# Experts taken in the order of their token counts, with a room of their own rank each (gate loop attention, then top-1 routed experts)

## The chip, the cores and the metric

The kernel runs on one core of one Trainium2 chip. The metric is the device time of one execution in microseconds (us), the median of several executions. The profile is of one execution; its span runs from the first to the last instruction, and its own time is a little longer than the span.

## What is computed

The first half is a gated linear recurrence, 4 batches of 8 heads, 768 tokens, head size 48. The second half sends each of the 3072 tokens (384 values) to one of 8 experts.

```python
for t in range(S):                       # attention
    new_re = ar * S_re - ai * S_im;  new_im = ar * S_im + ai * S_re
    S_re, S_im = (new_re + kv, new_im)
    y[:, :, t] = einsum('bhd,bhde->bhe', q[:, :, t], S_re)
logits = x @ w_gate                      # x: (3072, 384), 8 experts
expert_idx = argmax(logits, axis=1);  gate_w = probs[arange(N), expert_idx]
for e in range(E):                       # w1[e]: (384, 1024), w2[e]: (1024, 384)
    out[mask] = gate_w[mask, None] * (maximum(x[mask] @ w1[e], 0) @ w2[e])
```

## The kernel before

**Two stages.** In the attention stage (`front`, `chunk`, `route`) the work is cut into units of 128 to 384 tokens. ScalarE (ACT) and VectorE (DVE) turn gates, queries and keys of a unit into the operand `zp`; SyncE (SP) moves it by DMA into `hz`; then TensorE (PE) works through chunks of 128 tokens. When enough chunks are done, `route` finds each token's expert and its place in that expert's room, and GpSimd (POOL) scatters the rows to the DRAM buffer `xs_hbm` (L495). Every expert has a room of `CAP` = 448 rows there; rows from `MINC` = 256 on are filled beforehand with empty rows by three DMAs (L528).

**The expert stage.** For expert e, `weights` loads the two weight matrices (`w1b`, `w2b`, 1536 KB each, three buffers of each), `tokens` loads the expert's room in four DMAs (`xb`, L617), and DVE transposes it into `xrt` (L629). Then come 8 groups of 3 matmuls, each 448 columns wide (L644), into one of five PSUM banks; ACT and DVE in turn apply the relu and write `ht`. The second matmul (L658) works in three tiles of 128 tokens, 8 matmuls of 384 columns each. The last 64 rows of two neighbouring experts share one tile (L670): the two experts' matmuls write the two halves of the output's 128 partitions. Each output tile is scaled by its gate on DVE (L602) and scattered to the output by POOL (L591).

**What sets the order.** Both stages are lists of operations with guessed durations in a `Plan`; `Plan.order` tries list schedules with random priorities, keeps the one with the shortest guessed span, and the instructions are issued in that order, engine by engine. ACT holds one table at a time; the attention plan has two kinds of ACT operation, and at each change of kind a table is loaded (L540). The plan of the expert stage starts where the attention plan ends; on SP the first weight loads stand after the last `hz` DMA.

**The guard.** From the final counts and some bounds the kernel computes a flag (`again`, L544 to L568). If an expert has more rows than its room or fewer than `MINC`, a slow path (from L691) computes everything again. It isn't run with these inputs: the final counts of the eight experts, worked out from the reference, are 354, 406, 392, 388, 370, 421, 338 and 403.

Of the kernel before, what the change touches and what calls it, by code (L numbers as in the profile page):

```python
# [30 lines left out]
CAP = 448  # L31
# [3 lines left out]
NB = CAP // 32  # L35
# [12 lines left out]
class Plan:  # L48
# [48 lines left out]
    def run(self, prio, edges, ins, back, stick):  # L97


        ops, n = self.ops, [len(x) for x in ins]  # L100
        ready, start = [0.0] * len(ops), [0.0] * len(ops)
        cur, dma = None, 0.0
        port, other = {"DVE": 0.0, "POOL": 0.0}, {"DVE": "POOL", "POOL": "DVE"}
        free, cand = {o["eng"]: 0.0 for o in ops}, {o["eng"]: [] for o in ops}
        for o in ops:
            if n[o["i"]] == 0:
                cand[o["eng"]].append(o["i"])
        for _ in ops:
            pick = None
            for eng, cs in cand.items():  # L110
                if not cs:
                    continue
                f = free[eng]
                fp = max(f, port[other[eng]]) if eng in port else f
                at = [max(fp if ops[i]["port"] else f, ready[i]) for i in cs]
                low = min(at)
                if pick is not None and low >= pick[2]:
                    continue
                best = None
                for i, t in zip(cs, at):  # L120
                    if t <= low + self.SLACK:
                        sw = ops[i]["tag"] and cur and ops[i]["tag"] != cur
                        key = prio[i] - (stick if sw else 0.0)
                        if best is None or key > best[0]:
                            best = (key, i, t + (self.TBL if sw else 0.0))
                if pick is None or best[2] < pick[2]:
                    pick = (eng, best[1], best[2])
            eng, i, t = pick
            o = ops[i]
            cand[eng].remove(i)  # L130
            start[i] = t
            free[eng] = issued = end = t + o["dur"] * (self.PE[t > self.PE[2] or back] if eng == "PE" else 1.0)
            if o["port"]:
                port[eng] = end
            cur = o["tag"] or cur
            if o["wire"] and not back:
                dma = end = max(dma, end) + o["wire"]
            for s, us, data in edges[i]:
                ready[s] = max(ready[s], end + us + (ops[s]["wire"] if back else 0.0) if data else issued)
                n[s] -= 1  # L140
                if n[s] == 0:
                    cand[ops[s]["eng"]].append(s)
        return start, max(free.values())
# [19 lines left out]
def gateloop_then_moe(ctx, tc, gates, qk, v, wg, w1, w2, out):  # L163
# [50 lines left out]
    ones_b = const([128, 128], "ones_b", 1.0, BF16)  # L214
    cum = const([128, E], "cum")
# [7 lines left out]
    with ExitStack() as att:  # L223
# [277 lines left out]

        def setup():
# [14 lines left out]
        with tc.manual_schedule():  # L517
            for u in range(NU):
# [7 lines left out]
                if u == 3:  # L526
                    for h in range(3):
                        P.add("SP", 0.65, lambda h=h: nc.sync.dma_start(  # L528
                            xs_hbm.rearrange("(e s) w -> s e w", e=E)[MINC + 64 * h:MINC + 64 * h + 64],
                            bc(empty[0:64, None, :], [64, E, W])), (), (("empty", h),), lat=2, wire=3.2, after=moved[1])  # L530
                for c in range(t0 // 128, t1 // 128):
                    chunk(b, c, t1 - t0 == TU)
                    for r0, r1 in ROUTES[b]:
                        if r1 == c + 1:
                            route(b, r0, r1)
            for i in P.order():
                o = P.ops[i]
                if o["tag"] and o["tag"] != getattr(P, "cur", None):
                    P.cur = o["tag"]
                    nc.scalar.preload_act_table_set("natural_log_exp_and_others" if P.cur == "LE" else "trig_and_small")  # L540
                o["fn"]()
# [20 lines left out]
    nc.vector.tensor_scalar(out=f4, in0=f4, scalar1=float(CAP), scalar2=None, op0=ALU.is_le)  # L562
# [8 lines left out]
    with ExitStack() as ms:  # L571
# [4 lines left out]
        NW = 3  # L576
        w1b = buf("w1b", NW, [128, DT * F])
        w2b = buf("w2b", NW, [128, FT * DM])
        xrt = buf("xrt", 2, [128, DT, CAP])
        ht = buf("ht", 2, [128, FT, CAP])  # L580
        yo = buf("yo", 4, [128, DM])
        hg = buf("hg", 2, [128, 2])
        xb = buf("xb", 2, [128, NB, 96])
        gi = buf("gi", 2, [128, 3, 2])
        HB, OB = bank[0:5], bank[5:8]
        M = Plan()
# [19 lines left out]
        def weights(e):  # L606
            ws = e % NW
            M.add("SP", 0.65, lambda: nc.sync.dma_start(w1b[ws], w1[e * 128:e * 128 + 128, :]), (), (("w1", ws),), lat=1.9, wire=5.2,
                  after=rows[-1:])
            M.add("SP", 0.65, lambda: nc.sync.dma_start(w2b[ws], w2[e * 128:e * 128 + 128, :]), (), (("w2", ws),), lat=1.9, wire=5.2,  # L610
                  after=rows[-1:])

        def tokens(e, s):

            for i in range(4):
                eng, dma = ("ACT", nc.scalar) if e == 0 and i % 2 else ("SP", nc.sync)
                j = M.add(eng, 0.65, lambda i=i, dma=dma: dma.dma_start(  # L617
                    xb[s][32 * i:32 * i + 32], xs_hbm[e * CAP:(e + 1) * CAP, 104 * i:104 * i + 96].rearrange("(j p) w -> p j w", p=32)),
                    ("routed",), (("xb", s, i),), lat=2.5 if e == 0 else 6.0, wire=0.9)
            if e:  # L620
                rows.append(j)
            z, hgi = e % 2, e // 2 % 2
            M.add("SP", 0.65, lambda: nc.sync.dma_start(
                gi[s], xs_hbm[e * CAP:e * CAP + 384, XW:W].rearrange("(j p) w -> p j w", p=128)), ("routed",), (("gi", s),), lat=3.0, wire=0.5)
            M.add("SP", 0.65, lambda: nc.sync.dma_start(
                hg[hgi][64 * z:64 * z + 64], xs_hbm[e * CAP + 384:(e + 1) * CAP, XW:W]), ("routed",), (("hg", hgi, z),), lat=3.0, wire=0.1)
            for j in range(4):
                b0, b1 = 4 * j, min(4 * j + 4, NB)
                M.add("DVE", (b1 - b0) * 96 * 0.00105 + 0.1, lambda b0=b0, b1=b1: nc.vector.transpose(  # L629
                    xrt[s][:, :, 32 * b0:32 * b1].rearrange("p d (b t) -> p b d t", t=32),  # L630
                    xb[s][:, b0:b1].rearrange("p b (d c) -> p b d c", d=DT)), tuple(("xb", s, i) for i in range(4)), (("xrt", s, j),))

        def expert(e):
            s, ws = e % 2, e % NW
            if e > 1:
                weights(e)
            tokens(e, s)
            for f_ in range(FT):
                hb = (e * FT + f_) % 5

                def f(f_=f_, hb=hb):
                    for d in range(DT):
                        c = d * F + f_ * 128
                        nc.tensor.matmul(HB[hb][:, 0:CAP], lhsT=w1b[ws][:, c:c + 128], rhs=xrt[s][:, d, :], start=(d == 0), stop=(d == DT - 1))  # L644
                M.add("PE", 2.28, f, (("w1", ws),) + tuple(("xrt", s, j) for j in range(4)), (("H", hb),))
                if f_ % 2:
                    M.add("DVE", 0.6, lambda f_=f_, hb=hb: nc.vector.tensor_scalar_max(ht[s][:, f_, :], HB[hb][:, 0:CAP], 0.0),  # L647
                          (("H", hb),), (("ht", s, f_),))
                else:
                    M.add("ACT", 0.6, lambda f_=f_, hb=hb: nc.scalar.activation(ht[s][:, f_, :], HB[hb][:, 0:CAP], func=ACT.Relu),  # L650
                          (("H", hb),), (("ht", s, f_),))
            for j in range(3):
                ob = cnt["o"] % 3
                cnt["o"] += 1
                for a in range(2):
                    def f(j=j, ob=ob, a=a):
                        for f_ in range(4 * a, 4 * a + 4):
                            nc.tensor.matmul(OB[ob][:, 0:DM], lhsT=ht[s][:, f_, j * 128:j * 128 + 128], rhs=w2b[ws][:, f_ * DM:f_ * DM + DM],  # L658
                                             start=(f_ == 0), stop=(f_ == FT - 1))
                    M.add("PE", 2.6, f, (("w2", ws),) + tuple(("ht", s, f_) for f_ in range(4 * a, 4 * a + 4)), (("O", ob),))  # L660
                finish(ob, gi[s][:, j, 0:1], gi[s].bitcast(I32)[:, j, 1:2], (("gi", s),))
            hgi = (e // 2) % 2
            if e % 2:
                ob = cnt["o"] % 3
                cnt["o"] += 1

                def f(ob=ob):
                    for f_ in range(FT):
                        for z in range(2):
                            nc.tensor.matmul(OB[ob][64 * z:64 * z + 64, 0:DM], lhsT=ht[z][:, f_, 384:CAP],  # L670
                                             rhs=w2b[(e - 1 + z) % NW][:, f_ * DM:f_ * DM + DM], start=(f_ == 0), stop=(f_ == FT - 1),
                                             skip_group_check=True)
                rd = tuple(("ht", z, f_) for z in range(2) for f_ in range(FT)) + (("w2", (e - 1) % NW), ("w2", e % NW))
                M.add("PE", 5.3, f, rd, (("O", ob),))
                finish(ob, hg[hgi][:, 0:1], hg[hgi].bitcast(I32)[:, 1:2], (("hg", hgi, 0), ("hg", hgi, 1)))

        with tc.manual_schedule():
            weights(0)
            weights(1)
# [162 lines left out]
```

## Time and profile before

| what | value |
|---|---|
| three runs, median (lowest to highest) | 575.65 us (570.49 to 575.82) |
| profiled execution, its own time | 571.32 us |
| its span | 569.6 us, mean granted TensorE clock 0.927 |
| busy: PE, DVE, ACT, POOL | 477.8, 280.2, 184.1, 113.2 us |
| first L644 matmul starts | 271.62 us |
| last scatter (L591) starts | 564.38 us |

Busy time is a mean over two stages with different limits, so the stages are read apart below: which engine is full in each, and what the others wait for.

### The profile page before, as it was taken

What the parts mean: (1) busy time and instruction counts of PE and PEld (TensorE: products, weight loads), DVE (VectorE), ACT (ScalarE), POOL (GpSimd) and SP (SyncE); (2) the same over time, 40 slices, a digit from 0 to 9 for tenths busy, and PEclk for the clock granted to TensorE, in tenths of its full rate; (3) what the DMA queues carried; (4) which work ended last, traced back from release to release, by engine and by line L of the source; (5) the groups of instructions that cost most, each with busy time, mean ns of one, the idle gap of its engine ahead of it and who ended that gap; (6) DMA issues with size and microseconds to landing.
All of it is one profiled execution on the core that took longest, in us unless ns stands there. A gap on an engine that the chain in (4) does not pass through costs nothing. (4 is left out here: it accounts for less than half of the span.)

```text
span 569.6 us, 6957 instructions
## 1 busy us (share of the span) xinstructions
PE 477.8 (84%) x2689; PEld 324.0 (57%) x2689; DVE 280.2 (49%) x449; ACT 184.1 (32%) x259; POOL 113.2 (20%) x116
## 2 busy tenths in 40 slices
PE   0254766988697989881999999999999999999995
PEld 0244666877696878780455545555455554555552
DVE  7999999999899999342212021022011120200201
ACT  6784776767586756240100000100000000000100
POOL 6342214026303521421000001010021010100202
PEclk9966868898799889896899999999999999999999
DMA  8755675759999664695936063067343300400101
GB/s 275 222 187 149 194 221 154 226 148 312 266 260 223 182 175 112 235 397 120 274 71 159 28 171 138 3 239 181 52 152 126 111 29 1 138 14 0 47 10 48
DMA packets 48424, 86.15 MB, mean 151 GB/s; under 512 B 22512, under 2 KB 37904, under 8 KB 46336
## 3 DMA queue, kind: packets, MB, share of 16 engines
q1 hardware_dynamic: 43840, 75.19, 45.7%
q0 software_dynamic: 3328, 9.86, 4.7%
q10 hardware_dynamic: 1216, 0.59, 0.5%
q8 instruction: 23, 0.38, 0.3%
q14 instruction: 17, 0.14, 0.1%
HBM read 54.32 MB, written 13.21 MB: 119 GB/s over the span
## 5 line engine op out<-in xcount | busy, mean ns | idle before, releaser
L644 PE MATMUL bank<-xrt,w1b 128*128 128x448 f32 x384 | 150.1, 544 | 9.5 <-DVE xrt L629 9.5
L658 PE MATMUL bank<-w2b,ht 128*128 128x384 f32 x384 | 128.4, 487 | 0.0
L644 PEld LDWEIGHTS bank<-xrt,w1b 128*128 128x128 f32 x384 | 73.5, 192 | 78.9 <-issue 63.0
L658 PEld LDWEIGHTS bank<-w2b,ht 128*128 128x128 f32 x384 | 72.7, 190 | 54.3 <-issue 10.3
L400 PE MATMUL bank<-hz 128*128 128x128 f32 x384 | 65.1, 325 | 45.3 <-DMA hz<-zp 33.0
L650 ACT ACTIVATE ht<-bank 128x448 f32<-128x448 f32 x32 | 17.4, 545 | 253.9 <-PE bank L644 227.2
L400 PEld LDWEIGHTS bank<-hz 128*128 128x128 f32 x384 | 57.7, 231 | 50.1 <-DVE cs L330 25.3
L591 POOL DMA_INDIRECT out_dram<-yo,gi x24 | 23.5, 980 | 270.5 <-DVE yo L602 245.5
L647 DVE TENSOR_SCALAR ht<-bank 128x448 f32<-128x448 f32 x32 | 20.0, 624 | 93.9 <-PE bank L644 89.5
L602 DVE TENSOR_SCALAR yo<-bank,gi 128x384 f32<-128x384 f32 x24 | 14.8, 617 | 96.6 <-PE bank L658 91.8
L176 DVE TENSOR_TENSOR zp<-Z,cs 128x1152 f32<-128x1152 f32 (+2 forms) x40 | 45.2, 1169 | 0.1
L176 POOL TENSOR_TENSOR AB<-AB,C 128x1152 f32<-128x1152 f32 (+2 forms) x9 | 21.2, 2352 | 96.9 <-ACT C L264 89.7
L176 DVE TENSOR_TENSOR am<-bank,causal 128x512 f32<-128x512 f32 x48 | 32.0, 681 | 16.8 <-PE bank L400 10.8
L419 PE MATMUL bank<-am,v 128*48 128x128 f32 x384 | 30.4, 297 | 9.4 <-DVE am L176 9.2
L435 PE MATMUL bank<-turn,yt 128*128 128x104 f32 x192 | 29.2, 300 | 10.7 <-ACT yt L423 7.8
L495 POOL DMA_INDIRECT xs_hbm<-xg,slot x24 | 27.7, 1154 | 36.4 <-issue 14.9
L629 DVE STREAM_TRANSPOSE xrt<-xb 128x384 f32<-128x384 f32 (+1 forms) x32 | 14.0, 497 | 40.2 <-PE bank L644 32.7
L435 PEld LDWEIGHTS bank<-turn,yt 128*128 128x128 f32 x192 | 25.8, 209 | 13.1 <-ACT yt L423 8.5
L427 PE MATMUL bank<-v,kt 128*96 128x48 f32 x320 | 32.3, 257 | 0.0
L427 PEld LDWEIGHTS bank<-v,kt 128*96 128x96 f32 x320 | 30.7, 174 | 1.8 <-issue 1.5
L176 POOL TENSOR_TENSOR Z<-Z,AB 128x1152 f32<-128x1152 f32 (+2 forms) x9 | 21.7, 2407 | 41.8 <-ACT AB L264 41.7
L540 ACT ACT_TABLE_LOAD x23 | 29.5, 1283 | 1.2 <-PEq L830 0.8
(111 smaller groups left out, 479.1 us busy)
## 6 DMA issues: line engine op xcount, KB each, us to landing
w1b<-in_w_dram SPq DMA_DIRECT2D x8, 1536.0 KB
w2b<-in_w_dram SPq DMA_DIRECT2D x8, 1536.0 KB
hz<-zp SPq DMA_DIRECT2D x24, 432.0 KB
AB<-in_gates_dram SPq DMA_DIRECT2D x12, 576.0 KB
Z<-in_qk_dram SPq DMA_DIRECT2D x12, 576.0 KB
xb<-xs_hbm SPq DMA_DIRECT2D x30, 168.0 KB
v<-in_v_dram SPq DMA_DIRECT2D x8, 576.0 KB
xs_hbm<-empty SPq DMA_DIRECT2D x3, 836.0 KB
```

What stands on the lines that cost most here:

```text
L176: (eng or nc.vector).tensor_tensor(out=o, in0=a, in1=b, op=op)
L400: nc.tensor.matmul(SC[hf][:, (h % 4) * 128:(h % 4) * 128 + 128], lhsT=hk[:, h], rhs=hq[:, h], start=True, stop=True)
L419: nc.tensor.matmul(YT[ps, (h // 2) * 128:(h // 2) * 128 + 128], lhsT=V[:, cl, h * D:h * D + D], rhs=am[2 * par + hf][:, h % 4, :], start=( ...
L427: nc.tensor.matmul(ST[0:96, h * D:h * D + D], lhsT=kt[par][:, h * 96:h * 96 + 96], rhs=V[:, cl, h * D:h * D + D], start=(c == 0 and h == 0 ...
L435: nc.tensor.matmul(XT[:, p * 104:p * 104 + 104], lhsT=yt[par][:, p * 128:p * 128 + 128], rhs=turn[:, p, :], start=True, stop=True)
L495: i = nc.gpsimd.indirect_dma_start(out=xs_hbm[:, :], out_offset=bass.IndirectOffsetOnAxis(ap=R[slot][:, c:c + 1], axis=0), in_=xg[:, (g0 + ...
L540: nc.scalar.preload_act_table_set("natural_log_exp_and_others" if P.cur == "LE" else "trig_and_small")
L591: i = nc.gpsimd.indirect_dma_start(out=out[:, :], out_offset=bass.IndirectOffsetOnAxis(ap=index, axis=0), in_=y, in_offset=None, bounds_ch ...
L644: nc.tensor.matmul(HB[hb][:, 0:CAP], lhsT=w1b[ws][:, c:c + 128], rhs=xrt[s][:, d, :], start=(d == 0), stop=(d == DT - 1))
L647: M.add("DVE", 0.6, lambda f_=f_, hb=hb: nc.vector.tensor_scalar_max(ht[s][:, f_, :], HB[hb][:, 0:CAP], 0.0), (("H", hb),), (("ht", s, f_),))
L650: M.add("ACT", 0.6, lambda f_=f_, hb=hb: nc.scalar.activation(ht[s][:, f_, :], HB[hb][:, 0:CAP], func=ACT.Relu), (("H", hb),), (("ht", s, ...
L658: nc.tensor.matmul(OB[ob][:, 0:DM], lhsT=ht[s][:, f_, j * 128:j * 128 + 128], rhs=w2b[ws][:, f_ * DM:f_ * DM + DM], start=(f_ == 0), stop= ...
```

## The change

Experts are taken in the order of their counts. A new function `ranks`, run when all but the last 384 tokens are routed, sorts the counts on DVE; the result `order` holds the expert of each rank. SP (and ACT for the first expert) loads the expert's number into a register, and the DMAs of weights, tokens and gates take their address from it. Each rank has its own room (`CAPS`): 480, 448, 416, 416, 416, 384, 384, 384; they are worked through in the turns 0, 2, 1, 3 to 7. The room in `xs_hbm` is 480 rows for every expert. Rows past 384 are collected 32 at a time from several experts in two shared tiles of four parts each (`SHARED`), one finished with the second turn and one with the fifth. There are four buffers of `w2b` and three of `ht`; `weights` is called for one expert ahead of the loop, not for two. The three DMAs of empty rows cover 224 rows in place of 192. The planner gets one more rule (`landed`): a transfer that SP or ACT issues starts when the eighth last one has landed. The guard compares the counts by rank with `CAPS`.

```diff
-CAP = 448
+CAP = 480
+CAPS = (480, 448, 416, 416, 416, 384, 384, 384)
+TURNS = (0, 2, 1, 3, 4, 5, 6, 7)
+SHARED = ((1, ((0, 384, 0), (0, 416, 32), (0, 448, 64), (1, 384, 96))), (4, ((2, 384, 0), (2, 416, 32), (3, 384, 64), (4, 384, 96))))
...
-                at = [max(fp if ops[i]["port"] else f, ready[i]) for i in cs]
+                at = [max(fp if ops[i]["port"] else f, ready[i], landed[-8] if ops[i]["wire"] and eng != "POOL" else 0.0) for i in cs]
...
+        def ranks():
+            cnt = bank[2][:, 440:440 + E]
+            P.add("PE", 0.3, lambda: nc.tensor.matmul(cnt, lhsT=ones_b, rhs=cumb, start=True, stop=True), ("cumb",), ("RT",))
...
+            dv(lambda: tt(key, cnt, keyb, ALU.subtract), ("RT",), ("key",))
+            dv(lambda: tt(tmp, bc(key[:, None, :], full), bc(key[:, :, None], full), ALU.is_le), ("key",), ("tmp",))
+            dv(lambda: nc.vector.tensor_reduce(above, tmp, axis=AX, op=ALU.add), ("tmp",), ("above",))
+            dv(lambda: tt(pick, bc(above[:, None, :], full), bc(rev[:, :, None], full), ALU.is_equal), ("above",), ("pick",))
+            dv(lambda: tt(tmp, pick, bc(e_f[:, None, :], full), ALU.mult), ("pick", "above"), ("tmp",))
...
+                    nc.vector.tensor_reduce(order, tmp, axis=AX, op=ALU.add)
...
+                            if b == B - 1 and r1 == 3:
+                                ranks()
...
-        NW = 3
+        NW, NV, NH = 3, 4, 3
...
         def weights(e):
...
+                which[e] = ds(nc.values_load(order[0:1, TURNS[e]:TURNS[e] + 1], engines=ENG[0:2 if e == 0 else 1], min_val=0, max_val=E - 1,
...
+            for wb, wv, nb, nm in ((w1b, w1v, NW, "w1"), (w2b, w2v, NV, "w2")):
+                first = M.add("SP", 0.65, lambda wb=wb, wv=wv, nb=nb: nc.sync.dma_start(wb[e % nb][:, None, :], wv[:, which[e], :]),
...
         def expert(e):
-            s, ws = e % 2, e % NW
+            s, n, h = e % 2, CAPS[TURNS[e]], e % NH
...
-                        nc.tensor.matmul(HB[hb][:, 0:CAP], lhsT=w1b[ws][:, c:c + 128], rhs=xrt[s][:, d, :], start=(d == 0), stop=(d == DT - 1))
+                        nc.tensor.matmul(HB[hb][:, 0:n], lhsT=w1b[e % NW][:, c:c + 128], rhs=xrt[s][:, d, 0:n], start=(d == 0), stop=(d == DT - 1))
...
+            for z, (turn_, parts) in enumerate(SHARED):
+                if turn_ == e:
+                    tiles.append((tuple((t, 32, c0, p0) for t, c0, p0 in parts), hg[z], tuple(("hg", z, p0) for t, c0, p0 in parts if c0 == 384)))
...
                         for f_ in range(4 * a, 4 * a + 4):
+                            for t, m, c0, p0 in parts:
+                                nc.tensor.matmul(OB[ob][p0:p0 + m, 0:DM], lhsT=ht[t % NH][:, f_, c0:c0 + m],
+                                                 rhs=w2b[t % NV][:, f_ * DM:f_ * DM + DM], start=(f_ == 0), stop=(f_ == FT - 1),
...
             weights(0)
-            weights(1)
```

## The prediction

> **What bounds the kernel now.** I first cut the span into stretches at the places where the engines change roles (after each stretch: its length, then busy us of PE, weight loads, DVE, ACT and POOL with instruction counts, granted PE clock, DMA share, GB/s).
>
> ```profile
> 0.00:230.00 230.00, 160.49 (x1513) 146.24 (x1513) 217.68 (x302) 156.14 (x205) 74.95 (x75) 0.86 0.71 206
> 230.00:264.00 34.00, 25.52 (x281) 22.73 (x280) 11.63 (x56) 10.55 (x22) 10.86 (x14) 0.91 0.74 279
> 264.00:291.00 27.00, 19.38 (x48) 9.74 (x49) 5.30 (x11) 2.18 (x4) 0.00 (x0) 0.80 0.95 218
> 291.00:564.00 273.00, 272.44 (x850) 145.33 (x848) 45.48 (x81) 15.25 (x28) 26.45 (x27) 1.00 0.29 86
> ```
>
> Up to 230 us DVE is the full engine: 217.7 of 230, idle for 12.3. From 230 to 264 nobody is full; the last chunks and the routing run down as a chain. From 291 PE is full (272.4 of 273) at clock 1.00, with DMA at 0.29: whatever takes a matmul away there shortens the run one for one. Next the groups with shapes kept apart (busy us, mean ns; then idle before):
>
> ```profile
> L644 PE MATMUL bank<-xrt,w1b 128*128 128x448 f32 x384 | 150.1, 544 | 9.5 <-DVE xrt L629 9.5
> L658 PE MATMUL bank<-w2b,ht 128*128 128x384 f32 x384 | 128.4, 487 | 0.0
> L540 ACT ACT_TABLE_LOAD x23 | 29.5, 1283 | 1.2 <-PEq L830 0.8
> L670 PE MATMUL bank<-w2b,ht 128*64 128x384 f32 x128 | 21.5, 489 | 0.0
> ```
>
> The mean is a matmul's latency, overlapped with the next, so it isn't its price. The price is the pace, which the timeline has (start, length, what):
>
> ```profile
> 320.00 5.32 PE L658 MATMUL bank<-w2b,ht 128*128 128x384 f32 x16
> 325.16 4.67 PE L644 MATMUL bank<-xrt,w1b 128*128 128x448 f32 x12
> 329.67 5.32 PE L658 MATMUL bank<-w2b,ht 128*128 128x384 f32 x16
> ...
> 337.18 0.20 PEld L670 LDWEIGHTS bank<-w2b,ht 128*64 128x64 f32 x4 [0.65 <-issue]
> 337.56 0.14 PEld L670 LDWEIGHTS bank<-w2b,ht 128*64 128x64 f32 x2 [0.18 <-issue]
> 337.88 0.14 PEld L670 LDWEIGHTS bank<-w2b,ht 128*64 128x64 f32 x2 [0.18 <-issue]
> ```
>
> From start to start, 16 records of 384 columns take 5.16 us, 0.3225 each; 12 of 448 take 4.51, 0.3758 each. Both are 0.839 ns a column, so the price goes with the columns. (A matmul here is two records: 192 matmuls, 384 records.) In the shared tile two 64-wide loads stand in 0.14 us though each takes 0.137, and the next pair comes 0.32 us later: two half-width matmuls cost one slot. The start of the expert stage is the last view:
>
> ```profile
> 264.16 6.31 SPq L617 DMA_DIRECT2D xb<-xs_hbm  x6
> ...
> 269.81 1.76 DVE L629 STREAM_TRANSPOSE xrt<-xb 128x384 f32<-128x384 f32 x4 [7.51 <-DMA xb<-xs_hbm]
> ...
> 271.62 19.86 PE L644 MATMUL bank<-xrt,w1b 128*128 128x448 f32 x48 [9.50 <-DVE xrt L629]
> ```
>
> It waits for the tokens, not for weights: the first loads of both experts were issued from 237.05 to 239.9, and the DMA share, 0.8 to 1.05 from 236 to 256, is 0.42 at 256 to 258, when they are through.
>
> **The change, part by part.**
>
> *First matmul, narrower.* 8 groups x 3 matmuls x 2 = 48 records an expert. Before: 8 x 48 x 0.3758 = 144.3 us. After: the widths add up to 3328 columns, not 3584: 48 x 3328 x 0.839 ns = 134.0. **-10.3.** It lies wholly in the full PE stretch. The relus of the same groups (L650 0.545, L647 0.624 us) are far shorter than a group (2.25), so they don't take over.
>
> *Shared tiles.* Before 4 tiles x 16 pairs x 0.3225 = 20.6 us. After 2 tiles with 8 x 4 x 2 = 64 records each, 32 wide. The trace has no 32-wide load. Lower end: four at once, 32 slots x 0.3225 = 10.3; a record of 384 columns is never quicker. Middle: matmuls at once but the loads in series at 0.137 us, 32 x 0.548 = 17.5. Upper end: nothing at once, 128 x 0.3225 = 41.3. I take 10.3, by the nearest row, L670, the same instruction with 64 columns, where loads and matmuls for different columns do run side by side. **-10.3** (ends -10.3 and +20.7). Entering a shared tile costs some 0.4 us (0.65 idle before the first load where 0.18 is usual); before there are four entries, after it three, since one of the two tiles is cut in two by other groups: nothing.
>
> The page "TensorE: Matmul & The Clock Gate", section "Measured speedup vs the span model", of the Trainium skill speaks against the full factor: four tiles side by side were measured there at 3.07 times, not 4. By that the two tiles would take 41.3 / 3.07 = 13.5 us and the kernel 3.2 more than my sum, an estimate from the page; no run here shows it, and the 64-wide row shows the full factor of 2.
>
> *Ranks.* One small matmul (0.17) and six DVE operations on up to 64 elements; the nearest rows are the routing's, 0.17 to 0.21 us, and 1.0 when DVE waits for its port beside POOL. 1.2 us, bounds 1.0 to 6. In the changed order they stand before the routing of the next two chunks; there DVE of before waits 5.4 us for PE (245.3 to 250.6). Hidden; without that cover +1.2.
>
> *Register loads.* A load of `again` takes 0.48 us on SP. The first one waits for `order`, so the first weight loads move from 237 to some 249 to 253 (the three chunks' routing ends at 245.3, the next starts at 252). Behind it on SP stand only the expert stage's own loads. Two matrices, 3.1 MB, at the 400 GB/s of 240 to 256 take 8 us: there at 261 or 262, ten before they are needed. Hidden; what is late next is the second expert's pair, now issued after the tokens, at about 270; the DMA has room for it by 280, and it is needed at about 291.
>
> *Transfers addressed by register* have no row of before. Lower end nothing; upper end one more issue of 0.5 us for each of the some 62 that SP does in 290 us, which is covered, except ahead of the first tokens: two there, +1. I take +0.5. Tokens of 15 blocks in place of 14 add 7% to the 5.3 us from issue to landing: +0.4. First expert's start: **+0.9.**
>
> *Guard.* Three more DVE operations, 0.5 us, in DVE's wait of 7.51 for the tokens. *Empty rows.* 0.43 MB more, about 1 us of DMA where the share falls to 0.01 (210 to 215 us). Nothing.
>
> *The attention stage's order.* The new planner rule reshuffles the whole stage; every engine's order differs. DVE's work stays the same, so the bound stays, and 12.3 us of idle is all that a better order could win. But ACT's list has 39 table loads in this stage, not 23: 16 x 1.283 = 20.5 us more on an engine that is busy for 156 of 230. It would be full for 177: still room, less slack in the chains where DVE waits for it. Bounds: -12 and +20.5. Idle and load being where they are, most of the extra falls into ACT's 74 us of idle; I take **+1**.
>
> **Sum.** -10.3 - 10.3 + 0.9 + 1 = -18.7, on the profiled execution's 571.32: 552.6. Three other runs have a median of 575.65; from there it would be 557. The executions lie in two groups, 570.5 to 571.3 and 575.7; I take **554**, nearer to the execution whose rows I used. Changes under 1% can't be told from none here.
>
> **Rivals.**
>
> *The new attention order costs 5 to 25 us.* For it: 16 more table loads, and ACT in chains with DVE up to 230 us. Against: in that time DVE waited for ACT for only 6 us in all (3.0 at L313, 2.3 at L451, 0.8 at L317 by the view of waits). 557 to 578, likeliest 563. Chance 0.20, of which 0.07 ends faster, 0.07 the same and 0.06 slower.
>
> *The four narrow matmuls don't run at once (slower).* One mechanism, in the two shared tiles: all 128 records in series, 41.3 for 20.6. Then 554 + 31 = 585. It decides from about 0.23 us a record, where 128 of them eat up the 10.3 won on the first matmul. For it: no 32-wide row. Against: L670. Chance 0.05. With the loads alone in series it is 561: 0.07.
>
> *The new order fits better.* DVE's 12.3 us of idle shrink to a few: 541 to 549. For it: PE waits 33 us for `hz` in this stage, and the new rule counts a limit on SP's transfers that the old plan left out. Against: DVE is 95% busy whatever PE waits for. Chance 0.08.
>
> *The ranks don't fit.* Of the first 2688 tokens the counts fall in the order 371, 361, 357, 342, 340, 325, 302, 290; the same experts end with 421, 406, 403, 392, 388, 370, 354, 338, all inside 480, 448, 416 (three times), 384 (three times). The slow path stays out; no chance given.
>
> Forecast: **554, chance 0.60**, its own range 547 to 562. Range with the rivals: 543 to 569. Faster by over 1% in the forecast, the better order, the loads in series and its part of the first rival: 0.60 + 0.08 + 0.07 + 0.07 = 0.82; the same 0.07; slower 0.06 + 0.05 = 0.11.
>
> **What will show it.** Right: the first matmul's records at a pace of 0.4027, 0.3758, 0.349 and 0.3225 us for its four widths; in the shared tiles four loads to a slot of 0.32; PE full from about 291 on; its first start at 271 to 275. Wrong: PE waiting for `w1b` or `w2b` in the expert stage; four narrow records taking well over 0.32 us; DVE's idle up to the last `zp` well above 12 us, with ACT as releaser; the attention stage's last scatter later than 266 us.

## The result, and the profile after

The changed kernel takes 574.77 us (median of 12 runs, 571.91 to 575.76), the kernel before on the same chip 571.29 us. The ratio is 1.0041, 95% interval 1.0017 to 1.0066: no gain, but 0.2 to 0.7% lost. 554 was forecast. The profiled execution took 575.67 us, its span is 573.9.

The same stretches as before, for the changed kernel (length, then busy us of PE, weight loads, DVE, ACT, POOL, granted clock, DMA share, GB/s):

```profile
0.00:230.00 230.00, 153.09 (x1392) 139.11 (x1393) 201.78 (x264) 170.25 (x209) 75.02 (x82) 0.84 0.69 202
230.00:264.00 34.00, 28.23 (x318) 26.13 (x315) 17.75 (x62) 14.08 (x28) 10.42 (x13) 0.90 0.34 109
264.00:291.00 27.00, 9.71 (x92) 7.92 (x91) 8.81 (x45) 3.16 (x8) 3.14 (x4) 0.67 0.77 216
291.00:564.00 273.00, 268.75 (x883) 148.57 (x882) 44.86 (x82) 16.54 (x32) 22.55 (x23) 0.98 0.34 108
```

DVE, full before (217.7 of 230), has now done only 201.8 us of work by 230: it stands 16 us more in the attention stage. The matmuls behind did get cheaper, as the changed kernel's timeline of PE shows (start, length):

```profile
350.24 2.42 PE L700 MATMUL bank<-xrt,w1b 128*128 128x448 f32 x6
352.59 2.79 PE L719 MATMUL bank<-w2b,ht 128*32 128x384 f32 x32
355.30 2.52 PE L700 MATMUL bank<-xrt,w1b 128*128 128x448 f32 x6
...
424.09 4.35 PE L700 MATMUL bank<-xrt,w1b 128*128 128x416 f32 x12
428.28 5.32 PE L719 MATMUL bank<-w2b,ht 128*128 128x384 f32 x16
```

From start to start, 12 records of 416 columns take 4.19 us, 0.349 each; 32 narrow records take 2.71, as much as 8 full ones and a little for the entry. Both prices are those of the forecast. The first start of the expert stage, its one gap and the last scatter:

```profile
289.24 19.42 PE L700 MATMUL bank<-xrt,w1b 128*128 128x480 f32 x42 [10.18 <-DVE xrt L685]
472.37 4.21 PE L700 MATMUL bank<-xrt,w1b 128*128 128x384 f32 x6 [4.25 <-DVE ht L703]
569.28 0.98 POOL L639 DMA_INDIRECT out_dram<-yo,gi  x1 [1.99 <-POOLq L740]
```

The first expert starts at 289.24, not 271.62: 17.6 us late. From there to the start of the last scatter it is 280.0 us instead of 292.8, and in that stretch PE has one gap that it didn't have before, 4.25 us at 468. So +17.6 and -12.7, and 0.6 less behind the last scatter: the profiled execution is 4.3 us longer than the one before.

Where do the 17.6 come from? First the attention stage's gap, in the timelines of DVE, ACT and SP (SP's lines are issues of DMAs):

```profile
187.70 0.21 DVE L181 TENSOR_TENSOR oh<-eq,m 128x48 bf16<-128x48 f32 x1
195.41 0.20 DVE L466 TENSOR_REDUCE sm<-ex 128x6 f32<-128x48 f32 x1 [7.51 <-ACT ex L476]
```
```profile
194.41 0.84 ACT L279 ACTIVATE AB<-AB 128x768 f32<-128x768 f32 x1 [13.92 <-DMA AB<-in_gates_dram]
```
```profile
153.94 0.53 SPq L312 DMA_DIRECT2D AB<-in_gates_dram  x1
154.51 0.52 SPq L312 DMA_DIRECT2D Z<-in_qk_dram  x1
155.28 22.91 SPq L563 DMA_DIRECT2D xs_hbm<-empty  x3
178.29 2.26 SPq L386 DMA_DIRECT2D v<-in_v_dram  x1
180.65 2.37 SPq L312 DMA_DIRECT2D AB<-in_gates_dram  x1
```

Read backwards. DVE names ACT as its releaser, but ACT itself stood 13.92 us for the second half of a unit's `AB`; that load was issued at 180.65, behind the three transfers of empty rows, whose issue took SP 22.91 us. In the kernel before the same three issues took 3.01:

```profile
151.72 3.01 SPq L528 DMA_DIRECT2D xs_hbm<-empty  x3
```

The DMA view of the changed kernel from 154 to 180 us, in 40 slices (busy tenths of the 16 DMA engines; GB/s):

```profile
DMA  9979996211111111111111111111214899987289
GB/s 225 224 165 314 370 370 269 96 48 49 51 49 46 46 46 46 46 44 46 44 46 46 46 44 46 46 44 49 69 46 134 232 247 286 260 221 162 72 250 268
```

For some 15 us the engines are busy for a little over one tenth (0.13 from 162 to 170 us in a table of stretches), at 46 GB/s: a share of 0.13 is what two busy engines of 16 would show. The transfers have 74, 75 and 75 rows (224 in three parts); before they had 64 each.

### The profile page after: what moved, and what is told of

The parts are those of the page before. It is cut to its first block, busy times and chain, and to the rows that moved or that the text cites. A ratio compares the mean times of both kernels' runs of the same rounds, so it can differ in the third digit from the quotient of the medians.

```text
span 573.9 us, 7113 instructions
## 1 busy us (share of the span) xinstructions
PE 464.1 (81%) x2690; PEld 324.0 (56%) x2690; DVE 273.8 (48%) x452; ACT 204.0 (36%) x275; POOL 114.1 (20%) x125
## 5 line engine op out<-in xcount | busy, mean ns | idle before, releaser
L700 PE MATMUL bank<-xrt,w1b 128*128 128x416 f32 (+3 forms) x384 | 143.0, 526 | 14.4 <-DVE xrt L685 10.2
L719 PE MATMUL bank<-w2b,ht 128*128 128x384 f32 (+1 forms) x512 | 139.5, 489 | 0.0
L700 PEld LDWEIGHTS bank<-xrt,w1b 128*128 128x128 f32 x384 | 74.4, 195 | 77.3 <-issue 40.9
L719 PEld LDWEIGHTS bank<-w2b,ht 128*128 128x128 f32 (+1 forms) x512 | 77.3, 171 | 59.8 <-issue 13.0
L706 ACT ACTIVATE ht<-bank 128x416 f32<-128x416 f32 (+3 forms) x32 | 16.5, 517 | 262.9 <-PE bank L700 256.2
L415 PE MATMUL bank<-hz 128*128 128x128 f32 x384 | 61.7, 316 | 41.8 <-DVE zp L181 36.7
L415 PEld LDWEIGHTS bank<-hz 128*128 128x128 f32 x384 | 55.2, 223 | 45.5 <-DVE chk L324 36.7
L703 DVE TENSOR_SCALAR ht<-bank 128x416 f32<-128x416 f32 (+3 forms) x32 | 18.8, 590 | 112.3 <-PE bank L700 107.2
L181 DVE TENSOR_TENSOR zp<-Z,cs 128x1152 f32<-128x1152 f32 (+2 forms) x40 | 47.2, 1209 | 0.3
L442 PE MATMUL bank<-v,kt 128*96 128x48 f32 x320 | 33.6, 262 | 12.7 <-ACT kt L410 12.4
L181 POOL TENSOR_TENSOR AB<-AB,C 128x1152 f32<-128x1152 f32 (+2 forms) x9 | 22.8, 2539 | 64.2 <-ACT C L279 40.3
L450 PE MATMUL bank<-turn,yt 128*128 128x104 f32 x192 | 31.4, 315 | 5.0 <-ACT yt L438 2.7
L427 PE MATMUL bank<-hz,sb 128*48 128x128 f32 x320 | 26.2, 316 | 10.4 <-ACT yt L438 5.9
```

Source lines behind the costliest of these rows:

```text
L181: (eng or nc.vector).tensor_tensor(out=o, in0=a, in1=b, op=op)
L415: nc.tensor.matmul(SC[hf][:, (h % 4) * 128:(h % 4) * 128 + 128], lhsT=hk[:, h], rhs=hq[:, h], start=True, stop=True)
L427: nc.tensor.matmul(YT[ps, (h // 2) * 128:(h // 2) * 128 + 128], lhsT=sb[1 - par][:, h * D:h * D + D], rhs=hq[:, h], start=(h < 2), stop=Fa ...
L442: nc.tensor.matmul(ST[0:96, h * D:h * D + D], lhsT=kt[par][:, h * 96:h * 96 + 96], rhs=V[:, cl, h * D:h * D + D], start=(c == 0 and h == 0 ...
L450: nc.tensor.matmul(XT[:, p * 104:p * 104 + 104], lhsT=yt[par][:, p * 128:p * 128 + 128], rhs=turn[:, p, :], start=True, stop=True)
L700: nc.tensor.matmul(HB[hb][:, 0:n], lhsT=w1b[e % NW][:, c:c + 128], rhs=xrt[s][:, d, 0:n], start=(d == 0), stop=(d == DT - 1))
```

## The experiments

**Theory 1:** the expert stage's gain is real, and the first empty-row transfer, spread over two DMA engines only, holds everything behind it on SP. **Rival 1:** the new attention order with its 39 table loads costs it. **Rival 2:** ranks and registers do. A kernel was compared with the kernel before run beside it on the same chip; that kernel's medians lay between 569.4 and 572.2.

### The counts of rows, in both kernels

```diff
-                        h0, h1 = (MINC + (CAP - MINC) * x // 3 for x in (h, h + 1))
+                        h0, h1 = (256, 320, 400, 480)[h:h + 2]      # 64, 80, 80 rows
```

> The changed kernel with one thing altered: the three transfers of empty rows cover 64, 80 and 80 rows instead of 74, 75 and 75; same bytes, same order of every instruction. Theory 1 (the first transfer, 74 rows, runs on 2 of the 16 DMA engines: in the changed kernel's trace the DMA share is 0.13 and 45 GB/s from 160 to 174 us, and 967 KB at 45 GB/s are 21 us; the second half of a unit's AB stands behind it and DVE waits about 11.6 us): with a first count of 64, as before, the share stays near 1, the gap in DVE at 188 to 199 us closes, and the time falls by 9 to 12 us, to 563 to 566. Rival 1 (the new order with its 16 more table loads costs the time): the gap stays in its main part; 572 to 576. Rival 2 (the late ranks and registers cost it): no change, since they lie behind; 573 to 576.

Measured: **555.88 us, ratio 0.975 (0.971 to 0.979)**. SP's timeline has the three issues in 3.77 us, and the DMA view of 154 to 180 us is full:

```profile
155.78 3.77 SPq L563 DMA_DIRECT2D xs_hbm<-empty  x3
```
```profile
DMA  7889999999999999999999997887897210027999
GB/s 184 175 181 210 350 395 377 330 336 306 229 218 172 221 226 255 252 250 268 286 314 305 263 268 189 232 289 219 199 338 249 90 37 24 14 27 217 340 283 269
```

The first expert starts at 270.61 instead of 289.24, with the order of every instruction, the bytes, the ranks and all 39 table loads unchanged, and DVE has no gap left between 175 and 215 us. That the time fell 7 us below the range I expected has a reason: I had priced DVE's gap alone. From the end of the last `zp` to the first expert matmul the changed kernel needs 46.7 us, this one 40.9 and the kernel before 40.3; so the 6 us that the tail had lost, with POOL's scatters bunched between 250 and 261, belong to the same cause. Along which chain they were lost I did not follow.

The reverse, in the kernel before: 62, 65 and 65 rows for three times 64, the same 192 rows in all.

```diff
-xs_hbm...[MINC + 64 * h:MINC + 64 * h + 64], bc(empty[0:64, None, :], [64, E, W])
+xs_hbm...[(256, 318, 383, 448)[h]:(256, 318, 383, 448)[h + 1]], bc(empty[0:(62, 65, 65)[h], None, :], ...)
```

> The kernel before with one thing altered: its 192 empty rows go in transfers of 62, 65 and 65 rows instead of three of 64. Theory 1: the first one, 829 KB, runs on 2 engines at 45 GB/s for 18 us, the share falls to about 0.13 there, and AB and v behind it come late; the kernel before gets slower by 3 to 13 us (its next loads of AB stand right behind, but the unit they are for is a little later than in the changed kernel), 574 to 584. Rivals 1 and 2: the same bytes, so no change, 571 to 572.

Measured: **586.38 us, ratio 1.0285 (1.023 to 1.034)**, 17 us lost by the medians (569.38 before) where I had bounded it at 13. ACT's timeline has the same wait, longer, and DVE stands behind it for 17.02 us:

```profile
192.17 0.84 ACT L264 ACTIVATE AB<-AB 128x768 f32<-128x768 f32 x1 [21.94 <-DMA AB<-in_gates_dram]
```

Is it "not a multiple of 16", or the divisor? Two more counts in the changed kernel:

```diff
+                        h0, h1 = (256, 326, 396, 480)[h:h + 2]      # 70, 70, 84 rows
+                        h0, h1 = (256, 332, 400, 480)[h:h + 2]      # another run: 76, 68, 80 rows
```

> The changed kernel with transfers of 70, 70 and 84 empty rows in place of 74, 75 and 75; order of every instruction the same. Theory 1a (a transfer of n rows is spread over the largest number up to 16 that divides n: 74 gives 2 engines, 64 and 80 give 16, 70 and 84 give 14): the DMA share stays at 14/16 or above through the empty rows, the gap in DVE is absent, 555 to 558. Rival 1b (only counts that are multiples of 16 are spread, all others are slow): share about 0.13 again and 572 to 577.

Measured: 553.91 us, ratio 0.970 (0.966 to 0.975), 1 us below the range of theory 1a.

> The changed kernel with transfers of 76, 68 and 80 empty rows; order of every instruction the same. Theory 1a (a transfer of n rows is spread over the largest number up to 16 that divides n): 76 and 68 go to 4 engines, so the DMA share is about 0.25 for some 20 us (1.93 MB at 4 times the 22.5 GB/s that one engine moved in the changed kernel, 90 GB/s), and the time is 568 to 576. Rival 1c (only 74, twice a prime, is bad): share near 1 and 554 to 558.

Measured: 575.08 us, ratio 1.0053 (1.002 to 1.009), like the changed kernel itself. The DMA views, 154 to 180 us, with 70, 70 and 84 rows and with 76, 68 and 80:

```profile
DMA  9999999898999999998888898995412799899897
```
```profile
DMA  9953222222222222222222324999987543859999
GB/s 282 399 195 155 100 93 93 90 93 90 95 90 93 93 93 93 87 93 93 90 95 90 115 93 147 280 268 293 293 229 167 129 111 103 183 182 362 353 318 251
```

46 GB/s for 74 and 62 rows, 93 for 76 and 68, full speed for 70, 84, 64 and 80. Rivals 1b and 1c fall. The largest divisors up to 16 of these counts are 2, 4, 14 and 16, and two or four engines moved some 23 GB/s each. Four engines cost as much as two here, because there two transfers are slow, not one.

The packets show the number more directly. The trace has the start and length of every DMA packet, so one can count how many of the 1672-byte packets were in flight at once on SP's queue. Over the first 12 us of these transfers the commonest number is 2 with a first count of 74 (for 10.5 us of the 12) and of 62 (10.2), 4 with 76 (9.1), 14 with 70 (4.8) and 16 with 64 (4.0). Behind that it is 15 for the 75 rows of the changed kernel and 13 for the 65 of the altered kernel before.

The Trainium skill, page "DMA: Bandwidth & Descriptors", section "Why a DMA increments its semaphore by 16 and not by 1", states this rule: a DMA runs on the largest number of engines up to 16 that divides the slowest dimension of both sides. By the packets in flight these runs agree with it at 2, 4, 13, 14, 15 and 16 engines.

### The planner's rule

> As the run with 64, 80 and 80 rows, and in addition the planner without its new rule (a transfer waits until the eighth last has landed), which puts the attention stage in yet another order with 15 fewer instructions on ACT. Theory 1: the order is worth little by itself, so within 6 us of the run with 64, 80 and 80 rows alone, either way. Rival 1: the new rule's order and its table loads cost 10 to 20 us, so this run is by 8 us or more faster than that one.

```diff
-at = [max(fp if ops[i]["port"] else f, ready[i], landed[-8] if ops[i]["wire"] and eng != "POOL" else 0.0) for i in cs]
+at = [max(fp if ops[i]["port"] else f, ready[i]) for i in cs]
```

Measured: 562.12 us, ratio 0.985 (0.980 to 0.991): 6.2 us slower than with the new rule, with 25 table loads for 39. Rival 1 falls: it asked for 8 us faster. Theory 1's bound of 6 us was too narrow by a little, so an order can be worth some 6 us.

> The kernel before with the planner's new rule alone (every engine's order in the attention stage changes; 9 more instructions on ACT). Theory 1: the order is worth little, 566 to 577. Rival 1: the new rule's order costs most of what the changed kernel lost ahead of the experts (17.6 us), so 580 to 590.

Measured: 568.89 us, ratio 0.998 (0.995 to 1.001). In the kernel before the rule costs nothing that can be measured, with 33 table loads for 23; in the changed one its order is the better of the two. Rival 1 falls.

### The gap in the expert stage

With 64, 80 and 80 rows the gap is still there, 4.36 us at 450. The timelines of PE, DVE and POOL in that run:

```profile
454.54 3.64 PE L700 MATMUL bank<-xrt,w1b 128*128 128x384 f32 x6 [4.36 <-DVE ht L703]
```

```profile
433.76 0.62 DVE L650 TENSOR_SCALAR yo<-bank,gi 128x384 f32<-128x384 f32 x1 [3.66 <-PE bank L719]
...
444.41 0.62 DVE L650 TENSOR_SCALAR yo<-bank,gi 128x384 f32<-128x384 f32 x1 [9.57 <-PE bank L719]
453.40 0.62 DVE L650 TENSOR_SCALAR yo<-bank,hg 128x384 f32<-128x384 f32 x1 [8.37 <-DMA out_dram<-yo,gi]
453.94 1.01 DVE L703 TENSOR_SCALAR ht<-bank 128x384 f32<-128x384 f32 x2
```
```profile
445.31 0.98 POOL L639 DMA_INDIRECT out_dram<-yo,gi  x1 [27.73 <-DVE yo L650]
446.59 0.98 POOL L639 DMA_INDIRECT out_dram<-yo,gi  x1 [0.31 <-issue]
```

POOL takes the scatters in the order of the tiles, but PE finished the tiles in another, so POOL stood 27.73 us for the output scaled at 444.41 while two others lay ready. The scaling at 453.40 needs the buffer of the scatter at 446.59, which landed some 6.7 us later, and two relus queue behind it on DVE.

```diff
-        yo = buf("yo", 4, [128, DM])          # and: yi = cnt["y"] % 4
+        yo = buf("yo", 8, [128, DM])          # and: yi = cnt["y"] % 8
```

> The run with 64, 80 and 80 rows, and eight buffers of yo in place of four; PE's order is the same. Theory 2 (PE's only gap in the expert stage, 4.36 us at 450 us, and the slow clock behind it, 1.5 us, come from DVE standing at the scaling of the shared tile, which waits for a buffer whose scatter POOL had issued late and which landed 6.7 us after its start under a load of two weight matrices): the gap is absent and the time is 549 to 551, ratio to the kernel before about 0.966. Rival 2 (the relus themselves, or the late load of gates gi at 453.5 us, hold PE): the gap stays within 1 us, 555 to 557.

Measured: **546.69 us, ratio 0.959 (0.956 to 0.963)**. The gap is gone, and the stage runs from 267.53 to the last scatter at 540.53: 273.0 us. The time is 2 us below the range of theory 2. Of the 9 us against four buffers the stage gives 6.4; the rest lies ahead of it, where the instructions are the same and executions differ by some 3 us (with 70, 70 and 84 rows the same list reached its first expert at 267.74).

The other way to the same end is to let the planner know of the landing:

```diff
-            M.add("POOL", 1.05, lambda: scatter(yo[yi], index), (("yo", yi),) + reads, ("scattered",), lat=0.0)
+            M.add("POOL", 1.05, lambda: scatter(yo[yi], index), (("yo", yi),) + reads, (), lat=6.0)
```

> The run with 64, 80 and 80 rows, four buffers of yo, but the planner of the expert stage counts 6 us from a scatter's start until its buffer is free (0 before) and may issue the scatters in any order. Theory 2: the plan spreads the scalings so that DVE isn't held, and the gap at 450 us is absent or below 1 us; 549 to 553. Rival 2: the gap stays, 555 to 557.

Measured: 551.03 us, ratio 0.965 (0.959 to 0.970), no gap, and a stage of 273.7 us. Theory 2 stands by both, and rival 2 falls.

### Ranks, registers and the scatters' landing

> The run with 64, 80 and 80 rows, with the experts' order written into the kernel as constants for these inputs: the sorting on DVE still runs, but no register is loaded from it and no transfer waits for it. Theory 3 (ranks and registers are hidden, as predicted): the first weights are issued some 7 us earlier (at about 236 us instead of 243.9), the first expert matmul still starts at 270 to 271 us because it waits for the tokens, and the time is 553 to 558 (the order of the expert stage changes a little with the shorter list on SP). Rival 3 (registers and late weights cost): the first start comes 3 us or more earlier and the time is 550 or less.

Measured: 551.00 us, ratio 0.967 (0.962 to 0.972). It didn't test what I meant: the planner put the first weights behind the tokens, at 256 us, not 236, and the first matmul waited for them. Even so it came 38.9 us after the last `zp`, two sooner than the 40.9 of the run with registers. (It starts at 264.49, not 270.61; the rest of these 6.1 us lies ahead of the last `zp`.) One line of DVE differs. With registers, eight buffers and weights issued at 241:

```profile
255.39 0.16 DVE L503 TENSOR_REDUCE slot<-z 128x1 int32<-128x8 f32 x1 [3.50 <-DMA xs_hbm<-xg,slot]
```

The last slots go into the tile that two earlier scatters still read. With the weights out of the way this wait is absent. So is it the ranks' lateness, or any meeting of weights and scatters? Two runs, both with eight buffers: a third slot tile, and constants with the weights right behind `hz`.

```diff
+            slot = f"slot{(b + (r0 > 0)) % 2}"; R[slot] = rt["slot2"][:, 0:n] if r0 == 5 else R[slot]
```

> The run with 64, 80 and 80 rows and eight buffers of yo, and in addition a third tile of slots for the last 128 tokens; the order of every instruction is the same. Theory 4 (the last slots wait 3.5 us, from 251.9 to 255.4 us, because they go into the tile that the two scatters before them read, and those land late under the 3.1 MB of weights that the ranks have pushed to 241 to 253 us; the last scatter and the tokens behind it are late by as much): the wait is gone, the last scatter is issued at about 252, the first expert matmul comes 36 to 37 us after the last zp instead of 39.7, and the time is 543 to 544.5. Rival 4 (the tokens wait for the landing of those two scatters anyway): the first matmul keeps its distance within 1 us, and the time is 546 to 547.

Measured: **544.67 us, ratio 0.956 (0.953 to 0.959)**, the best of all. The wait is gone, the last scatter goes out at 252.61 instead of 256.36, and the first expert starts 37.9 us after the last `zp` instead of 40.5 (the expectation put this at 39.7). Rival 4 falls. Distance and time are a little above what theory 4 gave. By the times alone the run can't be told from the one without the third tile (the intervals overlap); by the trace it is 2.6 us, and the four runs with the same attention order but without that tile lie between 40.5 and 41.2.

```diff
-                which[e] = ds(nc.values_load(order[0:1, TURNS[e]:TURNS[e] + 1], ...), 1)
+            which[e] = ds((5, 1, 7, 2, 3, 4, 0, 6)[TURNS[e]], 1)     # first weights issued ahead of the tokens
```

> The run with 64, 80 and 80 rows and eight buffers of yo, with the experts' order as constants for these inputs (the sorting still runs, nothing waits for it) and the first two weight matrices issued right behind the last transfer of hz. Theory 4: they are through before the last scatters, so the last slots don't wait, and the first expert matmul comes 36 to 37.5 us after the last zp; 542 to 545. That difference, some 3 us, is then what ranks and registers cost. Rival 3 (ranks and registers are hidden, as predicted): the distance stays at 39 to 40 us, 546 to 548.

Measured: 548.94 us, ratio 0.964 (0.960 to 0.968), distance 41.2 us. This half of theory 4 falls. Weights issued at 234 meet earlier scatters, as ACT's timeline shows:

```profile
243.12 0.51 ACT L453 COPY xg<-bank 128x416 f32<-128x416 f32 x1 [3.82 <-DMA xs_hbm<-xg,slot]
...
247.21 0.51 ACT L453 COPY xg<-bank 128x416 f32<-128x416 f32 x1 [2.32 <-DMA xs_hbm<-xg,slot]
```

At both places where the 3.1 MB met scatters, something waited for the landing: `slot` or `xg`. Behind the tokens they met none, but there the first matmul waited for them. Knowing the order sooner gained nothing with the weights issued early (548.94 against 546.69 us).

## Why the prediction was wrong, point by point

- **What failed is the step "Empty rows. 0.43 MB more, about 1 us of DMA ... Nothing."** It counted bytes and looked for a quiet stretch of the DMA. It did not look at the shape: 224 rows in three parts are 74, 75 and 75, not 64. The first of them ran on two DMA engines and held SP for 22.9 us. With 64, 80 and 80 rows the same kernel gained 2.9% (ratio 1.0041 to 0.975), some 17 us: that is the price of the term put at nothing. The step also named 210 to 215 us as cover, while the transfers stand at 155 on SP, right ahead of a unit's `AB`.
- **First matmul, -10.3, and shared tiles, -10.3.** Right, term by term: paces of 0.402 (22 records of 480 in 8.85 us), 0.376, 0.349 and 0.3225, and 2.71 us for 32 narrow records where 2.58 was forecast. The stage without its gap is 273.0 us against 292.8: -19.8 for -20.6. The factor for four narrow matmuls was the full 4 in the pace, and 3.8 with the entry into the tile (2.71 us for 32 records that would take 10.32 in series). The 3.07 that I weighed against it, from the page "TensorE: Matmul & The Clock Gate", section "Measured speedup vs the span model", was measured there on four row groups; for three column groups, nearer to this case, the same table has 2.38. Neither fits these runs, and the measurement decides.
- **PE full from 291.** Missed by one gap. In the changed kernel it cost 4.25 us and 2.9 more at the low clock behind it: the granted clock was 0.61 from 472.37 to 479.82 us (6 records in 4.00 us, 8 in 3.45, for 1.94 and 2.58). The forecast had a term for each matmul and none for the output buffers, whose use the new order of tiles changed.
- **The attention order, +1 with bounds -12 and +20.5.** The middle was right within the 3 us by which executions differ, the reason for the upper bound wrong: 39 table loads stayed in the run with 64, 80 and 80 rows, and its last `zp` starts at 229.2, before at 230.8. So it was luck that the first rival's span, 557 to 578, held the result: another mechanism put it there.
- **First expert's start, +0.9.** 270.61 against 271.62 with spread rows: -1.0, within what executions differ. Register-addressed transfers cost nothing that shows.
- **Ranks and registers, hidden.** Right as far as constants in their place gained nothing with the weights issued early. "There at 261 or 262, ten before they are needed" was true of the weights and missed the neighbours: their transfer delays the scatters' landing, worth 2.6 us by the third slot tile.
- **The signs that I named** (DVE's idle well above 12 us with ACT as releaser, last scatter past 266) came: DVE stood 28.6 us up to the last `zp`, 7.5 of them in one wait for ACT, and the scatter came at 277.75. But the releaser named was only the last link; ACT's own wait pointed to the DMA.

The change was forecast at -18.7 us. With 64, 80 and 80 rows it is -13.5 (569.38 to 555.88): what is missing is the gap, 4.36 us and 1.5 at the low clock behind it. Without both faults it is -18.9 with the planner's count of the landing (551.03) and -23.2 with eight buffers (546.69), 19.8 of them in the expert stage and the rest ahead of it, where executions differ by 3: the forecast's mechanism holds in size.

## What to carry to other kernels

When a size changes, divide the new row count of every transfer, not only its bytes: a count with a large divisor up to 16 runs on many DMA engines, 74 or 62 on two, and what stands behind it on that queue waits. Follow a wait past the engine it names to that engine's own wait. When matmuls change their order, look at the buffers behind them: in-order scatters and their landing belong in the plan.

## What the hardware showed that I had not expected

- One DMA engine moved some 23 GB/s of these 1672-byte rows; a transfer confined to two of them held SP's issue of the next ones: 22.9 us for three DMAs that took 2.5 to 4.2 us when spread.
- A POOL scatter of 128 rows to `xs_hbm` landed 2.6 us after its issue at best, and 10.7 at worst (median 6.4, in the run with eight buffers); the planner counted 2.6.
- A pause of PE of some 4.3 us cost more behind it: 2.9 us of slow matmuls in the changed kernel, at a granted clock of 0.61, and 1.5 in the run with 64, 80 and 80 rows, at 0.76 from 454.54 to 460.59 us.
